# Experts' half pages become pages for at most 32 tokens, with fp32 products on four column groups of the array

## The chip, the cores and the metric

The kernel runs on one core of one Trainium2 chip. The metric is the device time of one execution in microseconds (us); the median of three runs before the change is 1147.6 us (1146.25 to 1148.35).

## What is computed

Three stages follow one another:

- attention over 4 batches, 8 heads, 768 positions, 64 dimensions, where a query sees 4 sink positions and a window of 128;
- a dense layer, `h = x @ w_in`, `g = h * cos(h)`, `g @ w_out`, on 3072 tokens, 512 wide inside and outside and 2048 wide between;
- a mixture of 8 experts with one expert per token: `logits = x @ w_gate + modality_bias[modality_id]`, the expert is the argmax, and `out = gate_w * (relu(x @ w1[e]) @ w2[e])`, with `w1[e]` 512 x 1024 and `w2[e]` 1024 x 512.

All inputs and outputs are float32. How many tokens an expert gets is known only on the chip. For the inputs as they are drawn, the reference sends 1 token to expert 2, 1549 to expert 4 and 1522 to expert 7, and none to the other five.

## The kernel before

Attention and the dense layer are interleaved and fill the first 830 us. The change touches only the experts' stage behind them.

**Pages.** A table computed on the chip (lines 1176 to 1262) cuts each expert's tokens into pages of 256. At most 19 pages exist (`NSUP`, line 99), and the program has code for each of them: `run(T)` (line 1305) nests itself, and each page stands under a condition that it is there. Page 0 and page 1 of the expert that led when it was chosen come first, then the rest of its pages, then the next experts in a ring. Row 2 of the table (line 1244) holds whether a page has more than 128 tokens. If it has, `run(T)` takes the full page, else the half page (`with full.Else()`, line 1353).

**Numbers.** A float32 operand is split into two fp32r parts, high and low, and a product is three fp32r matmuls (high by high, high by low, low by high). The weights of the current expert stand split in SBUF, 8 tiles each `w1h`, `w1l`, `w2h`, `w2l` of 128 x 512; the raw weights of the next expert wait in `rw1` and `rw2`. On the first page of an expert, `on_change` (line 1298) splits them: each split is one ACT copy (L1061) and one DVE subtraction (L148).

**A full page** (256 tokens): 8 blocks of `first_product` (line 1111), each 12 matmuls of 256 columns, relu on ACT (L1118) and the low part on DVE (L145); then `ahead`: the raw weights of the expert after (`reload`, line 1277, DMAs of SP), the next page's tokens transposed and split (`prelude`, line 1099, 8 transposes), and `second_product` (line 1140) for the first 128 tokens, 24 matmuls of 512 columns, between which the next page's `split_w1` stand; then the same product for the other 128 tokens. Each half ends with one ACT scaling by the gate weight (L1149) and one indirect DMA of POOL that scatters 128 rows into the output (L1152); rows that are padding are dropped by their index.

**A half page** (at most 128 tokens): `first_product_half` (line 1121) runs twice, for 512 of the 1024 hidden columns each. There the tokens are the stationary operand (128 columns) and the weights move: 12 matmuls of 512 columns. ACT takes the relu into `h_sb` (L1130), `turn_half` (line 1132) transposes it back in 8 transposes, and ACT (L1137) and DVE (L148) write 8 high and 8 low parts of 128 x 128. `ahead` with `second_product` for the first 128 rows ends the page.

**Order.** From line 1296 on the schedule is manual: every engine runs its instructions in the order in which the program text issues them. Conditions are evaluated by every engine on its own sequencer. On the half page the text says: the four `split_w2` of the first half on ACT and DVE before the first 12 matmuls, the other four before the second 12, then the transposes, the row indices of the page after next on DVE (`rows_ahead`, line 1316, six small operations), `reload`, `prelude` of the next page, and the second product with the next page's eight `split_w1`, the scaling, the gather of the page after next on POOL (`after`, line 1323) and the scatter.

Elsewhere in the kernel there are products in plain fp32, which the compiler issues as two passes, each with its own weight load: `po` in attention writes two column groups of 64 (tile 128*64), `ps` of the first attention pages uses two row groups of 64 (64*128), and `pf` the whole array.

Of the kernel before, what the change touches and what calls it, by code (L numbers as in the profile page):

```python
# [11 lines left out]
F32 = DT.float32  # L12
# [4 lines left out]
AF = mybir.ActivationFunctionType  # L17
ALU = mybir.AluOpType
AX = mybir.AxisListType

P = 128
# [34 lines left out]
WO_LAG = 1  # L56
CONV_A = 0.2
CONV_LEAD = 8


@with_exitstack
def kernel(
# [18 lines left out]
    NT, DM = out.shape  # L81
# [53 lines left out]
    def mm(o, l, r, start, stop):  # L135
        PE.matmul(o, l, r, start=start, stop=stop)  # L136

    def ts(e, o, i, s1, op0, s2=None, op1=None):
        if op1 is None:
            e.tensor_scalar(out=o, in0=i, scalar1=s1, scalar2=None, op0=op0)  # L140
        else:
            e.tensor_scalar(out=o, in0=i, scalar1=s1, scalar2=s2, op0=op0, op1=op1)  # L142
# [4 lines left out]
    def tt(e, o, a, b, op):  # L147
        e.tensor_tensor(out=o, in0=a, in1=b, op=op)  # L148
# [950 lines left out]
    def prelude(T, banks):  # L1099
        i = T % 2  # L1100
        yg = m_yg[i]
        xh, xl = m_x[i]
        for g in range(KD // 2):
            pt = banks[g].rearrange("p (c x) -> p c x", c=2)
            for c in range(2):
                for h in range(2):
                    PE.transpose(pt[:, c, h * P:(h + 1) * P], yg[h][:, (2 * g + c) * P:(2 * g + c + 1) * P], ident)  # L1107
            ACT.activation(out=xh[g], in_=pt, func=AF.Copy)
            tt(DVE, xl[g], pt, xh[g].bitcast(F32), ALU.subtract)
# [8 lines left out]
        ACT.activation(out=hT_h[f], in_=hp, func=AF.Relu)  # L1118
        stt(DVE, hT_l[f], hp, 0.0, hT_h[f].bitcast(F32), ALU.max, ALU.subtract)

    def first_product_half(T, g, hp):

        xh, xl = m_x[T % 2]
        for c in range(KD):
            i, o = divmod(c, 2)
            w = g * KD + c
            mm(hp, xh[i][:, o, 0:P], w1h[w], c == 0, False)
            mm(hp, xh[i][:, o, 0:P], w1l[w], False, False)
            mm(hp, xl[i][:, o, 0:P], w1h[w], False, c == KD - 1)
        ACT.activation(out=h_sb[g], in_=hp, func=AF.Relu)  # L1130

    def turn_half(g, pt):
        for o in range(KD):
            PE.transpose(pt[:, o * P:(o + 1) * P], h_sb[g][:, o * P:(o + 1) * P], ident)
        for o in range(KD):
            f, s = g * KD + o, slice(o * P, (o + 1) * P)
            ACT.activation(out=hT_h[f][:, 0:P], in_=pt[:, s], func=AF.Copy)  # L1137
            tt(DVE, hT_l[f][:, 0:P], pt[:, s], hT_h[f][:, 0:P].bitcast(F32), ALU.subtract)

    def second_product(T, h, yp, between=None, behind=None):  # L1140
        i = T % 2
        s = slice(h * P, (h + 1) * P)
        for f in range(KE):
            mm(yp, hT_h[f][:, s], w2h[f], f == 0, False)
            mm(yp, hT_h[f][:, s], w2l[f], False, False)
            mm(yp, hT_l[f][:, s], w2h[f], False, f == KE - 1)
            if between is not None:
                between(f)
        ACT.activation(out=m_ot[h], in_=yp, func=AF.Copy, scale=m_yg[i][h][:, DM:YC])  # L1149
        if behind is not None:  # L1150
            behind()
        POOL.indirect_dma_start(out=out[:, :], out_offset=bass.IndirectOffsetOnAxis(ap=m_ids[T % 4][:, h:h + 1], axis=0),  # L1152
                                in_=m_ot[h], in_offset=None, bounds_check=NT - 1, oob_is_err=False)
# [87 lines left out]
    ts(DVE, tab[:, 1], page, 0.0, ALU.is_equal)  # L1241
    tt(DVE, tab[:, 1], tab[:, 1], v1_, ALU.mult)
    stt(DVE, g1[:, :, 0], page, -256.0, pct, ALU.mult, ALU.add)
    ts(DVE, tab[:, 2], g1[:, :, 0], float(P), ALU.is_gt)
    tt(DVE, tab[:, 2], tab[:, 2], v1_, ALU.mult)
    ts(DVE, page, page, 2.0, ALU.mult)
    stt(DVE, page, pe_, float(NTI), page, ALU.mult, ALU.add)
# [18 lines left out]
    def maybe(cond):  # L1266
        return tc.If(cond) if cond is not None else ExitStack()
# [9 lines left out]
    def reload(T):  # L1277
        nxt = val(4, T, (ET.SP,), NE - 1)
        has = val(5, T, (ET.SP,), 1)
        load_raw(nxt, has > 0)  # L1280
# [10 lines left out]
        second_product(0, 1, m_y[1], lambda f: prelude(1, m_a) if f == PPF else None, lambda: gather_go(2))  # L1291
    m_h = [ps_h(f"m_h{i}") for i in range(2)]
    m_t = [m_y[1], ps_y(2, "m_t")]
    h_sb = [wpool.tile([P, 512], F32, name=f"h_sb{i}", tag=f"wo{KE + 6 + i}") for i in range(2)]

    ctx.enter_context(tc.manual_schedule())

    def on_change(T, f, split_f):

        if f % 2 == 0:  # L1300
            with tc.If(flags[T, "chg"] > 0):  # L1301
                split_f(f)
                split_f(f + 1)

    def run(T):
        more = T + 1 < NSUP
        cond = None
        if more:
            cond = flags.get((T + 1, "valid"))
            cond = cond > 0 if cond is not None else None  # L1310
            load_flags(T + 1)
        after = None
        cond2 = flags.get((T + 2, "valid"))
        cond2 = cond2 > 0 if cond2 is not None else None

        def rows_ahead():

            if T + 2 < NSUP:
                with maybe(cond2):
                    gather_rows(T + 2, val(3, T + 2, (ET.DVE,), NV - 1))  # L1320

        if T + 2 < NSUP:
            def after():
                with maybe(cond2):
                    gather_go(T + 2)

        def ahead(behind=None):
            if T > 1:
                reload(T)
            if more:  # L1330
                with maybe(cond):
                    prelude(T + 1, m_a)
            second_product(T, 0, m_y[0], (lambda f: on_change(T + 1, f, split_w1)) if more else None, behind)

        def split_ahead(f):
            if T > 1:
                on_change(T, f, split_w2)

        def look_ahead():
            if more:  # L1340
                tc.mark_branch_hint_location(f"full{T + 1}", hint=flags[T + 1, "full"], engines=(ET.PE,))
                if cond is not None:
                    tc.mark_branch_hint_location(f"more{T + 1}", hint=flags[T + 1, "valid"], engines=(ET.Pool, ET.Activation, ET.DVE))

        with tc.If(flags[T, "full"] > 0, preferred_fallthrough_block=True, label=f"full{T}" if T > 1 else None) as full:
            for f in range(KE):
                first_product(T, f, m_h[f % 2][:, 0:256])
                split_ahead(f)
            ahead()
            rows_ahead()  # L1350
            look_ahead()
            second_product(T, 1, m_y[1], None, after)
        with full.Else():
            for g in range(KE // KD):

                for f in range(g * KD, (g + 1) * KD):
                    split_ahead(f)
                first_product_half(T, g, m_h[g])
            for g in range(KE // KD):
                turn_half(g, m_t[g])  # L1360
            look_ahead()
            rows_ahead()
            ahead(after)
        if more and cond is not None:
            with tc.If(cond, preferred_fallthrough_block=True, label=f"more{T + 1}"):
                run(T + 1)
        return more and cond is None
# [40 lines left out]
```

## Time and profile before

| | |
|---|---|
| median of three runs | 1147.6 us |
| the profiled execution, its own time | 1148.82 us |
| its span, first to last instruction | 1147.0 us |
| mean granted TensorE clock over the span | 0.990 of full |
| PE busy | 1096.3 us (96%) |
| DVE busy | 716.0 us (62%) |
| ACT busy | 627.9 us (55%) |

The span is what the engines' records cover; the execution's own time has 1.8 us around it. A row of the timeline gives start and length in us, engine, line, operation, tiles (output from inputs), tile of the array, shape, and how many of a kind were merged; in brackets stand the idle time before it and what ended it. The granted clock is 1.00 at 2.4 GHz and 0.50 at 1.2 GHz.

### The profile page before, as it was taken

The numbers are of one execution on the slowest core, as the hardware profiler recorded it, in microseconds if no ns is written. First come the engines' busy times: TensorE is split into PE (matmuls) and PEld (weight loads), VectorE is DVE, ScalarE is ACT, GpSimd is POOL, SyncE is SP. The second block draws the span as 40 slices with busy tenths as digits, with TensorE's granted clock in tenths as the row PEclk, the third lists the DMA queues.
The fourth block names the chain that finished last, engine by engine and source line by source line (L and its number), as shares of the span: only waits on it lengthen the run. The fifth ranks groups of instructions, "written<-read, shape, count | busy, mean of one in ns | idle before, by whom it ended". The sixth has DMA issues, their size and how long they took to land.

```text
span 1147.0 us, 20828 instructions
## 1 busy us (share of the span) xinstructions
PE 1096.3 (96%) x6504; PEld 939.1 (82%) x6504; DVE 716.0 (62%) x2206; ACT 627.9 (55%) x1283; POOL 225.3 (20%) x275
## 2 busy tenths in 40 slices
PE   5989999999999999999999999999999998999995
PEld 3667778888888888888888889899889997899994
DVE  6678888877877777887787774746742225622210
ACT  4879888766676776666777653434322224522221
POOL 1232223211111121111111112321112211221110
PEclk9989999999999999999999999999999999999998
DMA  6557675433433432342343323623151114111110
GB/s 149 137 179 195 196 217 162 116 86 78 102 89 85 118 83 73 107 91 77 79 114 92 78 75 108 238 77 100 49 203 45 54 55 158 57 55 51 39 40 26
DMA packets 139285, 118.56 MB, mean 103 GB/s; under 512 B 96367, under 2 KB 105583, under 8 KB 139120
## 3 DMA queue, kind: packets, MB, share of 16 engines
q1 hardware_dynamic: 134800, 103.02, 32.1%
q0 software_dynamic: 4320, 13.65, 3.6%
q8 instruction: 65, 1.06, 0.4%
q14 instruction: 100, 0.82, 0.2%
HBM read 151.06 MB, written 19.67 MB: 149 GB/s over the span
## 4 chain that ended last, share of the span: by engine, by line
PE 75%; DVE 12%; DMA 4%; ACT 4%; issue 2%; POOL 1%; SPq 0%; ACTq 0%; POOLq 0%; DVEq 0%
PE hp L136 19%; PE y L640 17%; PE m_y L136 11%; PE m_h L136 10%; PE po L136 5%; PE ps L136 4%; DMA out_dram<-m_ot,m_ids 3%; PE pl L768 1%; DVE pT L148 1%; DVE ch L142 1%; DVE qT L148 1%; PE pt L570 1%; PE m_a L1107 1%; DVE kl L148 1%; DMA cv_in<-in_moe_w_in_dram 1%
## 5 line engine op out<-in xcount | busy, mean ns | idle before, releaser
L148 POOL TENSOR_TENSOR g_l<-ch,g_h 128x384 fp32r<-128x384 f32 x128 | 132.9, 1040 | 552.5 <-ACT g_h L712 513.6
L136 PE MATMUL hp<-xT_h,wi_h 128*128 128x384 f32 x512 | 182.8, 357 | 2.5 <-DVE ch L148 2.5
L136 PE MATMUL hp<-xT_l,wi_h 128*128 128x384 f32 x512 | 175.1, 342 | 0.0
L136 PE MATMUL hp<-xT_h,wi_l 128*128 128x384 f32 x512 | 174.4, 341 | 0.0
L640 PE MATMUL y<-wo,g_h 128*128 128x512 f32 x384 | 157.0, 410 | 0.0
L640 PE MATMUL y<-wo_l,g_h 128*128 128x512 f32 x384 | 155.9, 406 | 0.0
L640 PE MATMUL y<-wo,g_l 128*128 128x512 f32 x384 | 154.7, 403 | 0.2 <-POOL g_l L148 0.2
L702 ACT ACTIVATE ch<-ch,cols 128x384 f32<-128x384 f32 x128 | 78.8, 616 | 118.6 <-DVE ch L145 117.9
L136 PE MATMUL m_y<-wi_h,hT 128*128 128x512 f32 x416 | 133.6, 396 | 0.7 <-ACT m_ot L1149 0.5
L145 DVE SCALAR_TENSOR_TENSOR hT<-m_h,hT 128x256 fp32r<-128x256 f32 x88 | 37.3, 424 | 151.3 <-ACTq L1301 77.7
L136 PEld LDWEIGHTS hp<-xT_h,wi_h 128*128 128x128 f32 x512 | 97.2, 190 | 10.4 <-issue 3.4
L142 DVE TENSOR_SCALAR ch<-hp 128x384 int32<-128x384 f32 x128 | 71.0, 555 | 49.4 <-PE hp L136 38.0
L136 PEld LDWEIGHTS hp<-xT_l,wi_h 128*128 128x128 f32 x512 | 97.3, 190 | 5.5 <-issue 1.9
L136 PEld LDWEIGHTS hp<-xT_h,wi_l 128*128 128x128 f32 x512 | 96.9, 189 | 1.2 <-issue 0.9
L712 ACT ACTIVATE g_h<-ch 128x384 fp32r<-128x384 f32 x128 | 66.4, 520 | 54.0 <-DVE ch L148 42.9
L148 DVE TENSOR_TENSOR ch<-ch,hp 128x384 f32<-128x384 f32 x128 | 70.4, 551 | 38.1 <-ACT ch L702 37.7
L136 PEld LDWEIGHTS m_y<-wi_h,hT 128*128 128x128 f32 x416 | 78.9, 190 | 17.3 <-issue 0.9
L532 ACT ACTIVATE Pb<-Pb,mx 128x272 f32<-128x272 f32 (+1 forms) x168 | 82.8, 494 | 9.1 <-DVE mx L516 8.2
L640 PEld LDWEIGHTS y<-wo,g_l 128*128 128x128 f32 x384 | 72.3, 188 | 14.1 <-POOL g_l L148 0.6
L136 PE MATMUL m_y<-wi_l,hT 128*128 128x512 f32 x208 | 81.6, 392 | 0.0
L1118 ACT ACTIVATE hT<-m_h 128x256 fp32r<-128x256 f32 x88 | 33.7, 383 | 87.4 <-PE m_h L136 82.1
L640 PEld LDWEIGHTS y<-wo,g_h 128*128 128x128 f32 x384 | 72.4, 189 | 10.5 <-issue 2.7
(280 smaller groups left out, 2371.5 us busy)
## 6 DMA issues: line engine op xcount, KB each, us to landing
rw<-in_moe_w_dram SPq DMA_DIRECT2D x112, 512.0 KB
wo_l<-wl_scr SPq DMA_DIRECT2D x122, 256.0 KB
cv_in<-in_moe_w_in_dram SPq DMA_DIRECT2D x16, 512.0 KB
cv_out<-in_moe_w_out_dram SPq DMA_DIRECT2D x16, 512.0 KB
y_scr<-yt SPq DMA_DIRECT2D x24, 256.5 KB
xT_h<-xg_h SPq DMA_DIRECT2D x32, 192.0 KB
xT_l<-xg_l SPq DMA_DIRECT2D x32, 192.0 KB
qn<-in_q_dram SPq DMA_DIRECT2D x56, 96.0 KB
```

The costliest lines, as they stand in the source:

```text
L136: PE.matmul(o, l, r, start=start, stop=stop)
L142: e.tensor_scalar(out=o, in0=i, scalar1=s1, scalar2=s2, op0=op0, op1=op1)
L145: e.scalar_tensor_tensor(out=o, in0=i0, scalar=s, in1=i1, op0=op0, op1=op1)
L148: e.tensor_tensor(out=o, in0=a, in1=b, op=op)
L532: ACT.activation(out=Pb[t][j][:, c0:c1], in_=Pb[t][j][:, c0:c1], func=AF.Exp, scale=-1.0, bias=mx[:, i:i + 1], accum_out=sm[:, i:i + 1])
L570: PE.transpose(pt[:, j, P:2 * P], Pb[t][j][:, SEG:W3], ident)
L640: i = PE.matmul(o, l, r, start=start, stop=stop)
L702: ACT.activation(out=ch, in_=ch, func=AF.Sin, scale=TWO_PI, bias=half_pi)
L712: ACT.activation(out=gh, in_=ch, func=AF.Copy)
L768: return PE.matmul(pl[0][:, 0:NE], yT[:, c, :], wg[:, c, :], start=c == 0, stop=c == KD - 1)
L1107: PE.transpose(pt[:, c, h * P:(h + 1) * P], yg[h][:, (2 * g + c) * P:(2 * g + c + 1) * P], ident)
L1118: ACT.activation(out=hT_h[f], in_=hp, func=AF.Relu)
```

## The change

The limit between the two kinds of page falls from 128 to 32 tokens. A page of at most 32 tokens no longer uses `first_product_half`, `turn_half` and `second_product`. Its tokens (32 columns) are the stationary operand in each of four column groups of the array, the high and low parts of the tokens are added back to float32 on DVE, and the split weights are read as float32 and move in quarters: 256 of the 1024 hidden columns per group in the first product (32 calls), 128 of the 512 output columns per group in the second (64 calls). One relu, two transposes and one copy lie between, and four scalings (two on ACT, two on DVE) behind. The order of the text changes too: `few_first` stands ahead of the splits, `rows_ahead` and half of the next page's `split_w1` move behind the scaling and the scatter, and the gather of the page after next behind the scatter.

```diff
+FEW = 32
+GRP = P // FEW
...
-    def first_product_half(T, g, hp):
+    def few_first(T, hp):
 
         xh, xl = m_x[T % 2]
+        for g in range(KD // 2):
+            tt(DVE, x_few[:, 2 * g:2 * g + 2, :], xh[g][:, :, 0:FEW].bitcast(F32), xl[g][:, :, 0:FEW].bitcast(F32), ALU.add)
         for c in range(KD):
-            i, o = divmod(c, 2)
-            w = g * KD + c
-            mm(hp, xh[i][:, o, 0:P], w1h[w], c == 0, False)
-            mm(hp, xh[i][:, o, 0:P], w1l[w], False, False)
-            mm(hp, xl[i][:, o, 0:P], w1h[w], False, c == KD - 1)
-        ACT.activation(out=h_sb[g], in_=hp, func=AF.Relu)
-
-    def turn_half(g, pt):
-        for o in range(KD):
-            PE.transpose(pt[:, o * P:(o + 1) * P], h_sb[g][:, o * P:(o + 1) * P], ident)
-        for o in range(KD):
-            f, s = g * KD + o, slice(o * P, (o + 1) * P)
-            ACT.activation(out=hT_h[f][:, 0:P], in_=pt[:, s], func=AF.Copy)
-            tt(DVE, hT_l[f][:, 0:P], pt[:, s], hT_h[f][:, 0:P].bitcast(F32), ALU.subtract)
+            for ws in (w1h, w1l):
+                for j in range(GRP):
+                    w = ws[j // 2 * KD + c][:, j % 2 * 256:j % 2 * 256 + 256].bitcast(F32)
+                    mm(hp[j * FEW:(j + 1) * FEW, 0:256], x_few[:, c, :], w, c == 0 and ws is w1h, c == KD - 1 and ws is w1l)
+
+    def few_turn(hp, pt):
+        ACT.activation(out=h_few, in_=hp[:, 0:256], func=AF.Relu)
+        for o in range(2):
+            PE.transpose(pt[:, o * P:(o + 1) * P], h_few[:, o * P:(o + 1) * P], ident)
+        DVE.tensor_copy(ht_few, pt[:, 0:256])
+
+    def few_second(T, yp):
+        for f in range(KE):
+            ht = ht_few[:, f % 2 * P + f // 2 * FEW:f % 2 * P + (f // 2 + 1) * FEW]
+            for ws in (w2h, w2l):
+                for j in range(GRP):
+                    w = ws[f][:, j * P:(j + 1) * P].bitcast(F32)
+                    mm(yp[j * FEW:(j + 1) * FEW, 0:P], ht, w, f == 0 and ws is w2h, f == KE - 1 and ws is w2l)
+
+    def few_out(T, yp):
+        pr = m_yg[T % 2][0][0:FEW, DM:YC]
+        for j in range(GRP):
+            o, r = m_ot[0][0:FEW, j * P:(j + 1) * P], yp[j * FEW:(j + 1) * FEW, 0:P]
+            if j % 2 == 0:
+                ACT.activation(out=o, in_=r, func=AF.Copy, scale=pr)
+            else:
+                ts(DVE, o, r, pr, ALU.mult)
+        POOL.indirect_dma_start(out=out[:, :], out_offset=bass.IndirectOffsetOnAxis(ap=m_ids[T % 4][:, 0:1], axis=0),
+                                in_=m_ot[0], in_offset=None, bounds_check=NT - 1, oob_is_err=False)
...
-    ts(DVE, tab[:, 2], g1[:, :, 0], float(P), ALU.is_gt)
+    ts(DVE, tab[:, 2], g1[:, :, 0], float(FEW), ALU.is_gt)
...
-    h_sb = [wpool.tile([P, 512], F32, name=f"h_sb{i}", tag=f"wo{KE + 6 + i}") for i in range(2)]
+    h_few, ht_few = [wpool.tile([P, 256], F32, name=f"{n_}_few", tag=f"wo{KE + 6 + i}") for i, n_ in enumerate(("h", "ht"))]
+    x_few = fin.tile([P, KD, FEW], F32, name="x_few")
...
         with full.Else():
-            for g in range(KE // KD):
-
-                for f in range(g * KD, (g + 1) * KD):
-                    split_ahead(f)
-                first_product_half(T, g, m_h[g])
-            for g in range(KE // KD):
-                turn_half(g, m_t[g])
+            few_first(T, m_h[0])
+            for f in range(KD):
+                split_ahead(f)
+            few_turn(m_h[0], m_t[1])
+            for f in range(KD, KE):
+                split_ahead(f)
             look_ahead()
+            if T > 1:
+                reload(T)
+            if more:
+                with maybe(cond):
+                    prelude(T + 1, m_a)
+            few_second(T, m_y[0])
+            for f in range(KD if more else 0):
+                on_change(T + 1, f, split_w1)
+            few_out(T, m_y[0])
             rows_ahead()
-            ahead(after)
+            if after is not None:
+                after()
+            for f in range(KD, KE if more else 0):
+                on_change(T + 1, f, split_w1)
```

## Rows read from the trace of the kernel before

**Rows 1.** The chain that ended last, in order of time (start, us, what); its end
```profile
962.39 4.35 issue
...
981.95 11.90 PE m_h L136 x96
...
1101.36 36.30 DMA out_dram<-m_ot,m_ids
```

**Rows 2.** Stretches: length, busy us of PE PEld DVE ACT POOL, clock, DMA share, GB/s
```profile
937.91:961.23 23.32, 23.31 (x153) 21.07 (x151) 10.34 (x24) 9.70 (x20) 4.08 (x4) 1.00 0.21 65
961.23:982.00 20.77, 16.18 (x66) 13.29 (x67) 11.69 (x29) 13.05 (x29) 2.03 (x2) 0.84 0.59 212
971.19:978.02 6.83, 5.83 (x20) 5.15 (x21) 4.19 (x16) 4.45 (x14) 0.00 (x0) 0.50 0.80 270
1122.34:1136.45 14.11, 12.51 (x57) 9.78 (x56) 2.24 (x8) 4.57 (x12) 0.98 (x1) 1.00 0.07 26
```

**Rows 3.** DMA packets while the last scatter lands (1136 to 1147) and after 988.75
```profile
DMA packets 85, 0.08 MB, mean 7 GB/s; under 512 B 73, under 2 KB 73, under 8 KB 80
...
q0 software_dynamic: 80, 0.03, 0.9%
...
DMA packets 74, 0.00 MB, mean 2 GB/s; under 512 B 73, under 2 KB 73, under 8 KB 74
```

**Rows 4.** Timeline of page 13, the last one
```profile
1121.95 0.39 PE L136 MATMUL m_y<-wi_h,hT 128*128 128x512 f32 x1
1122.68 0.47 PE L136 MATMUL m_h<-wi_h,m_x 128*128 128x512 f32 x1 [0.34 <-issue]
...
1135.28 0.39 PE L136 MATMUL m_y<-wi_h,hT 128*128 128x512 f32 x1
1135.76 0.69 ACT L1149 ACTIVATE m_ot<-m_y,m_yg 128x512 f32<-128x512 f32 x1 [2.51 <-PE m_y L136]
```

**Rows 5.** Timeline of PE: fp32 products on two column groups, one group, whole array
```profile
307.59 0.54 PE L136 MATMUL po<-sp,vs_n 128*64 128x384 f32 x2
...
308.29 1.47 PE L136 MATMUL po<-pT,vn 128*64 128x128 f32 x16
...
308.29 0.39 PE L136 MATMUL po<-pT,vn 128*64 128x128 f32 x4
...
119.30 0.72 PE L136 MATMUL ps<-kT,qT 64*128 64x272 f32 x2
...
101.16 0.60 PE L136 MATMUL pf<-ident,pb_x 128*128 128x128 f32 x4
```

**Rows 6.** Groups by form (line, engine, operation, shapes, count, busy us, mean ns, idle before)
```profile
L136 PE MATMUL po<-pT,vn 128*64 128x128 f32 x168 | 16.7, 273 | 0.0
...
L1118 ACT ACTIVATE hT<-m_h 128x256 fp32r<-128x256 f32 x88 | 33.7, 383 | 87.4 <-PE m_h L136 82.1 <-DVEq L1301 2.8 <-issue 1.3
...
L145 DVE SCALAR_TENSOR_TENSOR hT<-m_h,hT 128x256 fp32r<-128x256 f32 x88 | 37.3, 424 | 151.3 <-ACTq L1301 77.7 <-ACT hT L1118 73.6
```

**Rows 7.** Timeline of page 6 and the start of page 7
```profile
962.58 0.47 PE L136 MATMUL m_h<-wi_h,m_xT_h 128*128 128x512 f32 x1 [1.35 <-ACT m_ot L1149]
...
966.90 2.19 ACT L1061 ACTIVATE wi_h<-rw 128x512 fp32r<-128x512 f32 x4 [4.96 <-issue]
...
967.57 5.06 DVE L148 TENSOR_TENSOR wi_l<-rw,wi_h 128x512 fp32r<-128x512 f32 x8 [9.94 <-ACT wi_h L1061]
...
969.63 0.66 PE L1134 MATMUL m_y<-ident,h_sb 128*128 128x128 f32 x4 [1.33 <-ACT h_sb L1130]
...
972.20 1.11 PE L1134 MATMUL m_t<-ident,h_sb 128*128 128x128 f32 x4 [1.91 <-ACT h_sb L1130]
...
974.67 0.78 PE L136 MATMUL m_y<-wi_h,hT 128*128 128x512 f32 x1
...
978.21 0.16 DVE L145 SCALAR_TENSOR_TENSOR m_ids<-m_it,m_ix 128x2 uint32<-128x2 f32 x1
...
981.78 0.40 PE L136 MATMUL m_h<-m_x,wi_h 128*128 128x256 f32 x2
```

More of the change, by code (lines that the diff above doesn't have):

```diff
@@ L1325, in after, with ahead @@
                     gather_go(T + 2)
-        def ahead(behind=None):
+        def ahead():
             if T > 1:
@@ L1332, in ahead @@
                     prelude(T + 1, m_a)
-            second_product(T, 0, m_y[0], (lambda f: on_change(T + 1, f, split_w1)) if more else None, behind)
+            second_product(T, 0, m_y[0], (lambda f: on_change(T + 1, f, split_w1)) if more else None)
         def split_ahead(f):
```

## The prediction

> **What bounds the kernel now.** I read the chain of waits first: in the experts' stage it is almost wholly PE, page after page (page 7's first product is one link of 11.90 us), and it ends with 36.3 us that the view gives to the last scatter, behind which the last page lies [rows 1]. Two stretches look different. Around 962 the chain is not PE for 4.35 us but "issue". The table of stretches says the same: a full page (937.91 to 961.23) keeps PE busy for 23.31 of 23.32 us, page 6 (961.23 to 982.00) for 16.18 of 20.77, with the clock at half for 6.83 us, and page 13 (1122.34 to the end of its scaling at 1136.45) for 12.51 of 14.11 [rows 2]. These two are the half pages, and the change can act on nothing else.
>
> **Do both pages become small ones?** Yes. The last scatter has 80 packets, of which 7 are over 2 KB, and the queue moved 0.03 MB in all: some 13 rows of 2 KB, not 128. After 988.75, where page 6's scatter ends, one packet over 512 B is left [rows 3]. The reference's routing agrees: expert 7's 1522 tokens are pages 0 to 5, expert 2's one token is page 6, and expert 4's 1549 are pages 7 to 13, the last with 13 tokens. No page holds 33 to 128 tokens, so none becomes a full page.
>
> **The price of a product.** A plain fp32 call is two passes. On the whole array four passes of 128 columns take 0.60 us, the last one 0.27 from its start, so a pass takes (0.60 - 0.27) / 3 = 0.11 us per 128 columns, 0.22 per 256 [rows 5, 6]. The passes of one call on one group follow each other: two of 272 columns take 0.72 us. Two column groups run side by side: two passes of 384 columns (0.33 each by that price) are both over after 0.54 us, where one after the other they would take 0.83, and 16 passes, half of 128 and half of 256 columns (the row bears the shape of the first), are over after 1.47 us, 1.30 without the drain of the last, where one after the other they would need 8 x 0.11 + 8 x 0.22 = 2.64 [rows 5]. Four groups are not in the trace. Bounds: as wide as two (each pass then counts half), or four wide (a quarter). I take four, because the second group costs no visible time in the rows, and keep two for the range. Then few_first, 32 calls or 64 passes of 256 columns, is 16 x 0.22 = 3.5 us; few_second, 64 calls or 128 passes of 128 columns, is 32 x 0.11 = 3.5 us. Each replaces 24 matmuls of 512 columns, some 5.5 us (the second product of page 13 ends its last start at 1135.28). A drain of some 0.17 us follows each product, as 0.27 for a pass of 0.11 shows [rows 4, 6].
>
> The Trainium skill, TensorE: Matmul & The Clock Gate (Part 3, The mechanism), says that matmuls start and end strictly in program order. By that rule a call's second pass would hold back the next group's first one, no more than two passes would ever overlap, and each product would cost 7.0 us instead of 3.5: that is the first rival below. The trace disagrees at the start of a series: two passes end within 0.54 us of the first start [rows 5], and they can't be those of one call.
>
> **Page 13, all of it on the path to the end.** From the end of page 12's product: branch 0.34 (kept, though the splits' branches now stand behind the product), few_first 3.5 + 0.17, relu 0.38 of 128 x 256 on ACT, two transposes 0.11 + 0.27, copy on DVE as the 128 x 256 row 0.42, few_second 3.5 + 0.17, two scalings each on ACT and DVE, some 0.5 together (one of 512 columns took 0.69), and four or five hand-overs of 0.05: 9.6 us [rows 4, 6]. Before: 14.1. **Gain 4.5 us**, since POOL's scatter waits for the scaling alone and all behind it (1147.0 - 1136.45 = 10.55 us to the end of the span) stays. POOL's conditions, which now stand behind the scatter, lie beside the wait for its landing. The two small DVE additions for x_few come before PE needs them: DVE has been idle since page 13's tokens were split. ACT's eight relu and transpose copies and DVE's eight subtractions go; they were hidden but for the first.
>
> **Page 6, with the splits of a new expert.** PE finishes few_first at 962.58 + 3.7 = 966.3, but nobody takes it: ACT comes out of its branch at 966.90 (an idle of 4.96 "issue" that the change leaves alone) and has four splits ahead of the relu, until 969.1 [rows 7]. So this product's gain is lost in a wait. Relu 969.5, transposes 969.95; DVE has its four subtractions behind it at 970.1 and copies until 970.5. Page 7's eight transposes, at 0.11 and a drain, end at 971.2. The clock: PE will have idled 3.2 us, as it idled 1.33 + 1.91 = 3.24 us in two parts before, when the records show half clock from 971.19 on [rows 2, 7]; I take the same here, and that it comes back after the products have run for as long as before, 978.02 - 974.67 = 3.35 us [rows 2, 7]. Half of few_second then runs at 0.22 per step (15 steps), 17 steps at 0.11 = 1.9: it ends at 976.6. The splits of w2 keep ahead of it (DVE is through at 972.95).
>
> Next late is DVE. ACT splits until 971.65; then come page 7's tokens, two copies on ACT and, at the price of two subtractions (5.06 / 8 = 0.63 each, 0.6 in a row), 1.3 us on DVE to 974.3, and four subtractions of w1 to 976.8 [rows 7], just in time for page 7's first block. Then stand on DVE, in order, two scalings (0.6), the row indices (register loads, which I put at 0.8, and six operations of 0.17 [rows 7]) and four more subtractions (2.4): the first hT_l of page 7 is done at 982.2. PE has two product banks, so its third block (a block is an eighth of some 11.6 us, 1.45) waits for it from 976.8 + 2.9 = 979.7: a new stall of 2.5 us, and 0.25 at the fourth block. ACT, with four splits behind its scalings, is ready sooner. Page 7's first product therefore starts 981.78 - 976.8 = 5.0 us sooner and waits 2.75 longer. **Gain 2.2 us**, which carries through, since from there every page is PE to the end. Bounds: full clock throughout gives 1.4 more; the clock lost again in the new stall costs up to 1.7 (half of 3.4), held down until 978.02 another 1.6. The gather for page 8 comes some 2 us earlier on POOL than before and isn't needed until 990; reload's DMAs on SP wait for the w2 splits as before, half a microsecond later, and are needed 8 us later.
>
> **Sum.** 4.5 + 2.2 = 6.7 us of the profiled 1148.8, which is 1.2 above the median; against the median 1147.6 - 6.7 = **1140.9 us**. About 0.2% (2.3 us) is what a measurement can tell from no change.
>
> **Rivals.** (1) Two groups wide. Products cost 7.0 each. Page 13: 9.6 + 7.0 = 16.6 against 14.1, a loss of 2.5. Page 6: few_first ends at 969.8, relu, transposes and page 7's transposes until 971.6, few_second until 978.8, page 7 starts 2.9 sooner and waits 2.75 longer, a gain of 0.1. Together 1150.0, slower than before; with half clock in page 7, 1151.7. It decides at a width under about 2.5 groups, where page 13 alone gains no more than 1.5 us. For it: no row has more than two. Against: the second group was free.
> (2) PE isn't fed fast enough. few_second is 256 instructions with its weight loads; the densest stretch of passes in the rows, four passes of 128 columns on two groups (two steps of 0.11, with four loads), is 0.027 us per instruction [rows 5]. At that pace few_second takes 6.9 us: page 13 gains 1.1, page 6 ends 1.7 later and gains 0.5, together 1146.0. For it: no denser stretch. Against: that one is paced by the array itself.
> (3) Page 7's stall and the clock eat page 6's gain: 0.5 to -1.1 instead of 2.2, so 1142.6 to 1144.2. For it: the stall is as long as the idle that cost the clock before.
> (4) The groups don't run side by side at all: 14 us per product, where 9.6 + 21 = 30.6 stands against 14.1; page 7 would start at 992.4, 10.6 later, and wait 2.75 more: 1147.6 + 16.5 + 13.4 = 1177.5. The rows for two groups speak against it.
>
> **How the numbers follow.** The forecast has 0.60 (1139 to 1142.6), rival 3 has 0.14, rival 1 0.13, rival 2 0.09, rival 4 and a stall in code loading that I don't see 0.04. Faster by over 0.2% is below 1145.3: 0.60 and most of rival 3, less 0.02 for what I don't see in either, 0.71. Same is 1145.3 to 1149.9: rival 2, over half of rival 1 (its price sits at the limit) and 0.01 of rival 3, 0.17. Slower: 0.12. The forecast's own range is 1139 (full clock, 1.4 more, and the branch saved) to 1142.6; with rivals 3, 2 and most of 1 the range is 1138.7 to 1150.0.
>
> **What would show it.** In the changed profile: in page 13, eight passes within some 0.25 us where now two to four stand, first product of about 3.7 us, last scaling some 4.5 us closer to page 12's end; in page 6, PE idle from 966.3 to 969.5, half clock from about 971; in page 7, an idle of 2 to 3 us before the third block, ended by DVE hT. Passes that start in pairs would prove rival 1, evenly spread starts at 0.05 us rival 2. The sum is wrong if page 7 has no stall, or if ACT reaches page 6 at another time.

## The result, and the profile after

The change made the kernel slower. The median went from 1146.92 us (1145.25 to 1148.35, four runs on the same chip) to 1161.05 us (1159.43 to 1161.95, four runs), a ratio on record of 1.0113 with a 95% interval of 1.0098 to 1.0128 (the two medians alone give 1.0123). The forecast was 1140.9 us, with a range that ended at 1150.0. Medians and ratios in this document leave out two executions that ran slower throughout at a lower clock, one of `few_act` (1204.25 us) and one of the kernel before beside it (1769.58 us).

The profiled execution took 1160.85 us, its span is 1159.1 us. The same view as [rows 2], for the changed kernel: page 5, page 6, a stretch of half clock in it, page 7, pages 7 to 12 (from the first scaling of page 7 to the last of page 12), page 13, the half clock in it, and what follows the last scaling.

```profile
936.77:960.06 23.29, 23.29 (x153) 21.05 (x151) 10.71 (x26) 9.74 (x20) 4.08 (x4) 1.00 0.20 61
960.06:981.60 21.54, 11.48 (x204) 7.68 (x203) 9.08 (x16) 8.75 (x17) 2.03 (x2) 0.76 0.60 207
969.11:972.47 3.36, 3.36 (x33) 1.91 (x36) 0.00 (x0) 0.00 (x0) 0.00 (x0) 0.50 0.85 241
981.60:1003.30 21.70, 19.36 (x133) 17.93 (x134) 14.25 (x36) 11.36 (x24) 3.98 (x3) 1.00 0.11 29
1002.60:1130.80 128.20, 123.12 (x784) 110.69 (x782) 27.37 (x76) 28.46 (x62) 21.39 (x21) 1.00 0.15 46
1130.71:1147.37 16.66, 10.52 (x194) 6.85 (x194) 1.11 (x3) 1.79 (x4) 0.98 (x1) 0.80 0.07 23
1134.12:1139.67 5.55, 5.52 (x53) 2.92 (x57) 0.00 (x0) 0.00 (x0) 0.00 (x0) 0.50 0.04 9
1147.37:1159.07 11.70, 0.00 (x0) 0.00 (x0) 0.00 (x1) 0.00 (x0) 0.99 (x1) 0.61 0.03 8
```

The row to stop at is the fifth. Pages 7 to 12 are all full and run not one instruction of the new code, yet they take 128.20 us. The kernel before needs 122.08 for the same 784 matmuls:

```profile
1000.30:1122.38 122.08, 122.04 (x784) 111.15 (x782) 27.04 (x74) 28.35 (x61) 21.37 (x21) 1.00 0.15 48
```

PE was never idle there before; now it idles 5.1 us, and its records are 1.1 us longer. The two small pages lost as well, where both should have gained: from page 5's last scaling to page 7's first 42.45 us (39.04 before), page 13 from page 12's last scaling to the end of its own 16.57 (14.07 before), and the rest of the span 11.70 (10.60). With the 6.12 of the full pages that is 3.41 + 6.12 + 2.50 + 1.10 = 13.1 us; the stretch up to page 5's last scaling was 1.1 shorter in this execution, so the spans differ by 12.0.

Where the full pages lose it is in a view that the busy times leave out: the branches of the condition "full page", by duration. Columns: engine, operation, count, shortest / median / longest in ns, first and last start in us. First the changed kernel, pages 7 to 12, then the kernel before:

```profile
L1365 PEldq COMPARE_BRANCH  x11: 71/3392/4186, 1003.7 to 1126.8; - x11
```

```profile
L1345 PEldq COMPARE_BRANCH  x11: 70/169/317, 1001.4 to 1118.4; - x11
```

Five of each are tests at a page's start (70 to 83 ns). The other six are the jumps with which a full page leaves its own code and skips the small page's: 0.17 to 0.32 us before, 3.4 to 4.2 us now, on PE's sequencer. The DMA view of the jump that starts at 1003.7 shows what arrives while it lasts, one packet of 16 KB on the queue "instruction":

```profile
q0 software_dynamic: 101, 0.35, 32.6%
q8 instruction: 1, 0.02, 1.8%
```

Each of the six jumps has such a packet, which starts 0.9 to 1.0 us behind the jump's start. In the same stretch of the kernel before (1001.4 to 1004.9) that queue has no packet. Over pages 7 to 12 it has 16 in the changed kernel and 10 in the kernel before, one more for each of the six jumps:

```profile
q8 instruction: 16, 0.26, 0.9%
```

```profile
q8 instruction: 10, 0.16, 0.6%
```

In page 7 PE's last matmul ends 4.2 us after the jump begins, so most of a jump is hidden behind matmuls that are queued: the six take 22.1 us together, and 6.1 show.

Page 6 and its successor, timeline of the changed kernel (as [rows 7]):

```profile
965.54 1.08 PE L138 MATMUL m_h<-wi_h,x_few 128*32 128x256 f32 x8 [5.48 <-issue]
965.89 2.19 ACT L1063 ACTIVATE wi_h<-rw 128x512 fp32r<-128x512 f32 x4 [5.05 <-issue]
969.11 0.65 PE L138 MATMUL m_h<-wi_l,x_few 128*32 128x256 f32 x4 [2.11 <-issue]
974.07 0.38 ACT L1135 ACTIVATE h_few<-m_h 128x256 f32<-128x256 f32 x1 [5.99 <-issue]
981.60 0.50 PE L138 MATMUL m_h<-m_x,wi_h 128*128 128x256 f32 x2 [1.65 <-issue]
987.07 0.50 PE L138 MATMUL m_h<-m_x,wi_h 128*128 128x256 f32 x2 [2.34 <-DVE hT L147]
```

PE stands 5.48 us before the page's first matmul and 2.11 us in the middle of the product, both put down to "issue", a wait for nothing that the profile shows. Ahead of the first matmul PE's sequencer is held by the branch into the page, 4.91 us from 960.4; in the middle there is no branch, but a packet of 16 KB on q8 (966.4 to 967.7), so that wait is put down to code by inference. Page 13 (as [rows 4]) opens the same way, though the view names ACT's sequencer for its 3.44 us, and then runs its first product at half clock:

```profile
1134.15 1.08 PE L138 MATMUL m_h<-wi_h,x_few 128*32 128x256 f32 x8 [3.44 <-ACTq L1321]
1134.97 1.11 PE L138 MATMUL m_h<-wi_l,x_few 128*32 128x256 f32 x8
...
1140.64 0.38 ACT L1135 ACTIVATE h_few<-m_h 128x256 f32<-128x256 f32 x1 [9.16 <-PE m_h L138]
...
1142.04 0.43 PE L138 MATMUL m_y<-wi_h,ht_few 128*32 128x128 f32 x8 [0.52 <-DVEq L1321]
1142.28 0.40 PE L138 MATMUL m_y<-wi_l,ht_few 128*32 128x128 f32 x8
...
1145.86 0.36 ACT L1153 ACTIVATE m_ot<-m_y,m_yg 32x128 f32<-32x128 f32 x1 [4.83 <-PE m_y L138]
1146.25 0.34 DVE L142 TENSOR_SCALAR m_ot<-m_y,m_yg 32x128 f32<-32x128 f32 x1 [4.27 <-ACT m_ot L1153]
1146.63 0.36 ACT L1153 ACTIVATE m_ot<-m_y,m_yg 32x128 f32<-32x128 f32 x1 [0.41 <-DVE m_ot L142]
1147.02 0.35 DVE L142 TENSOR_SCALAR m_ot<-m_y,m_yg 32x128 f32<-32x128 f32 x1 [0.43 <-ACT m_ot L1153]
```

### The profile page after: what moved, and what is told of

It reads as the page before. It is cut to its first block, busy times and chain, and to the rows that moved or that the text cites. A ratio compares the mean times of both kernels' runs of the same rounds, so it can differ in the third digit from the quotient of the medians.

```text
span 1159.1 us, 21349 instructions
## 1 busy us (share of the span) xinstructions
PE 1089.5 (94%) x6780; PEld 928.1 (80%) x6780; DVE 714.3 (62%) x2200; ACT 623.3 (54%) x1267; POOL 225.8 (19%) x275
## 4 chain that ended last, share of the span: by engine, by line
PE 72%; DVE 12%; issue 7%; ACT 4%; DMA 2%; POOL 1%; SPq 0%; POOLq 0%; DVEq 0%; ACTq 0%
PE hp L138 19%; PE y L642 18%; PE m_y L138 9%; PE m_h L138 9%; PE po L138 5%; PE ps L138 5%; PE pl L770 1%; DVE pT L150 1%; DVE ch L144 1%; DVE qT L150 1%; DVE kl L150 1%; DMA out_dram<-m_ot,m_ids 1%; PE pt L572 1%; DVE cv_a L147 1%; ACT Pb L534 1%
## 5 line engine op out<-in xcount | busy, mean ns | idle before, releaser
L138 PE MATMUL m_y<-wi_h,hT 128*128 128x512 f32 x384 | 122.1, 393 | 0.5 <-ACT m_ot L1168 0.5
L138 PEld LDWEIGHTS m_y<-wi_h,hT 128*128 128x128 f32 x384 | 72.0, 188 | 15.4 <-issue 0.9
L642 PEld LDWEIGHTS y<-wo_l,g_h 128*128 128x128 f32 x384 | 72.5, 189 | 9.1 <-DMA wo_l<-wl_scr 1.1
```

Of the source, the lines that this page charges most:

```text
L642: i = PE.matmul(o, l, r, start=start, stop=stop)
```

## The experiments

Theory C: PE's instructions come in pieces by DMA, and the longer code of the small pages makes every jump over it, and every entry into it, wait for a piece. Rival O: the new order of the small pages, or their transfers, does it. The table collects all kernels by stretch, each from the scalings in its timeline: A from page 5's last scaling to page 7's first, B from there to page 12's last, C from there to the end of page 13's last, D to the end of the span.

| kernel | A | B | C | D | median us, ratio to before (95%) |
|---|---|---|---|---|---|
| before | 39.04 | 122.08 | 14.07 | 10.60 | 1146.92 |
| after | 42.45 | 128.20 | 16.57 | 11.70 | 1161.05, 1.0113 (1.0098 to 1.0128) |
| pad_else | 39.10 | 128.20 | 14.25 | 10.99 | 1153.28, 1.0046 (1.0032 to 1.0059) |
| pad_356 | 38.86 | 124.10 | 14.62 | 10.97 | 1150.15 (one run) |
| pad_260 | 38.80 | 122.10 | 14.51 | 11.24 | 1146.45 (one run) |
| few_6_13 | 37.96 | 122.18 | 11.55 | 11.66 | 1144.83, 0.9977 (0.9966 to 0.9989) |
| half_5_12 | 39.49 | 127.81 | 10.83 | 11.69 | 1150.83 (one run) |
| few_fall | 38.51 | 122.15 | 10.46 | 12.78 | 1144.98, 0.9973 (0.9960 to 0.9987) |
| before_fall | 35.88 | 122.09 | 13.46 | 13.02 | 1146.23, 0.9983 (0.9969 to 0.9996) |
| few_tail | 36.48 | 122.08 | 12.50 | 10.27 | 1142.02, 0.9943 (0.9926 to 0.9961) |
| few_act | 37.20 | 122.09 | 12.44 | 10.15 | 1142.58, 0.9947 (0.9934 to 0.9960) |
| few_two | 37.20 | 122.08 | 11.95 | 10.06 | 1140.29 (one run) |
| few_mix | 38.05 | 122.11 | 13.76 | 10.76 | 1145.21, 0.9987 (0.9972 to 1.0002) |

The kernel before took 1147.55 to 1148.94 us in the median beside these runs. A row's stretches are those of one execution; where the code is the same they differ by up to 0.7 us (A of few_tail, few_act and few_two, D of the kernel before and pad_260).

**The jumped code alone.**

```diff
-        for c in range(KD):
+        for c in list(range(KD)) * times:
...
-                first_product_half(T, g, m_h[g])
+                first_product_half(T, g, m_h[g], 1 if T in (6, 13) else 7)
```

> The kernel before, in which the half page of every page except 6 and 13 issues its 24 matmuls of the first product seven times. These pages are all full or absent, so nothing more is executed; only the stretch of PE instructions that a full page jumps over at its end grows from about 164 to about 451, the length it has in the changed kernel (448). Theory C (code): a jump over the long stretch lands on instructions that are not loaded, 3.4 to 4.2 us instead of 0.17 to 0.33, of which some 0.5 to 2.3 us per page shows. Pages 7 to 12 then lose 5 to 7 us together, and the jump of page 5 delays the branch into page 6 by up to 2 us: 1152 to 1156 us. Rival O (order): the full pages of the changed kernel lose time to the new order of its small pages or to its DMAs: 1147 us, no change here.

B is 128.20 us, to the hundredth the changed kernel's, with not one instruction more executed:

```profile
998.56:1126.76 128.20, 123.10 (x784) 110.69 (x782) 27.02 (x74) 28.34 (x61) 21.37 (x21) 1.00 0.14 47
```

Five of the six jumps took 3.3 to 4.2 us, the sixth 0.43:

```profile
L1345 PEldq COMPARE_BRANCH  x11: 71/428/4184, 999.7 to 1122.8; - x11
```

Queue q8 has 17 packets in this stretch, against 10 in the kernel before; only PE's code was changed, so q8 brings PE's code. Rival O is out for the full pages: the length of code that PE skips is enough. A stayed as it was, against the expectation, because here the jumps of pages 1 to 5 were still short (0.3 us); the changed kernel's are 0.29 to 0.39 us on pages 1 to 3, 1.30 on page 4 and over 3.3 from page 5 on.

**How long is too long.** The same with 3 and with 5 in place of 7.

> As pad_else, with the first product's matmuls issued three times instead of seven: the stretch jumped over has 260 PE instructions (164 in the kernel before, 451 in pad_else). Instructions come in pieces of 16 KB, and 16 KB are 256 of them at 64 bytes each. If what counts is whether the target lies in the piece that is loaded ahead, the jumps are free or nearly so: pages 7 to 12 take 122.1 to 123 us from the scaling of page 6's successor to page 12's last, jumps under 0.5 us. If the cost grows with the length, they take 122.1 + 6.1 x 96 / 287 = 124.1 us.

> As pad_260, with the matmuls issued five times: 356 PE instructions. If the piece loaded ahead counts, some pages' jumps are long (over 3 us) and others short (under 0.5 us), pages 7 to 12 take 123 to 127 us. If the cost grows with the length, every jump costs some, and they take 122.1 + 6.1 x 192 / 287 = 126.2 us.

The branches of pages 7 to 12, first with 260 instructions to skip, then with 356:

```profile
L1345 PEldq COMPARE_BRANCH  x11: 70/287/326, 997.9 to 1114.9; - x11
```

```profile
L1345 PEldq COMPARE_BRANCH  x11: 70/292/3839, 999.8 to 1118.8; - x11
```

With 260 every jump is free, B is 122.10. With 356 one jump of the six takes 3.84 us and the others 0.43 at most, and B is 2.0 longer. So the cost is not proportional to the length: on these pages a jump takes 0.43 us at most, or over 3.2. The Trainium skill, Advanced Engine Details and Errata (ISA Cache), says that an engine's code is held in lines of 16 KB, 256 instructions. The packets of 16 KB agree, and the three lengths fit a target that is free when it lies in the piece already loaded ahead. The compiled programs bear this out for the jumps out of the full pages. Cut them in pieces of 256 instructions (branch labels not counted, which leaves about 243 of the 260 and 338 of the 356; the first cut fitted once for all kernels): of 121 such jumps, in all kernels of the table but few_fall and before_fall, the 98 whose target lies in the same piece or the next took 0.43 us at most, and of the 23 that skip a whole piece 22 took 0.62 to 4.19 us. The one that doesn't fit is the sixth in pad_else. The fit was made afterwards and no run tested it, so the rule remains argued; the branches into pages 6 and 13 don't follow it, they took 1.4 to 5.2 us in all these kernels.

**The short code on all pages but two.**

```diff
         with full.Else():
-            few_page()
+            few_page() if T in (6, 13) else half_page()
```

Here `few_page` is the body that the change put there, `half_page` the one that it took away.

> The changed kernel, in which only pages 6 and 13 carry the code for few tokens; the other pages carry the old half page behind their condition, which they never take. Theory C: the jumps of the full pages are 0.17 to 0.33 us again, pages 7 to 12 give back about 6 us, and page 6 is entered up to 2 us earlier: 1152.5 to 1155.5 us. What is left against the kernel before, some 6 us, is the price of the two small pages themselves. Rival O: 1160 to 1162 us as the changed kernel.

B is 122.18 as expected, but the kernel came out at 1144.83 us, 7.7 us below the expected range and faster than the one before. I had counted only the full pages' 6 us as the code's. A (-4.5 us against the changed kernel) and C (-5.0) belong to it as well: page 13's first product starts with no idle ahead of it (a hole of 0.88 us follows in its middle), and runs eight passes of 256 columns in 0.43 us where the changed kernel, at half clock, needs 0.85.

**Only the pages ahead of the two small ones.**

```diff
-            few_page() if T in (6, 13) else half_page()
+            half_page() if T in (5, 12) else few_page()
```

> The changed kernel with the old half page behind the condition of pages 5 and 12 alone (never taken there), so that only the full pages just ahead of the two small pages have a short stretch to jump over. Theory C: the small pages lose because PE comes late to their branch, held up in the jump at the end of the page ahead: from page 5's last scaling to page 7's first the profile shows 38 us as in few_6_13, not 42.4; page 13 takes 11.5 to 12.5 us, not 16.6, its first product at full clock. Pages 8 to 11 still pay 4 to 6 us in their jumps. In all 1150 to 1153 us. Rival: the small pages lose in their own code, whatever stands ahead of them: 42.4 and 16.6 us stay, 1159 to 1161 us.

B still pays (127.81), and page 13 is cured (10.83) though its own code is that of the changed kernel. So page 13, and page 6 for the greater part, lost by what stands ahead of them. The branch into page 13 takes about as long in both kernels, 2.05 us in the changed one and 1.93 here. In the changed kernel the jump out of page 12 (3.66 us) holds PE's sequencer, and the branch starts at 1131.8, when the last matmul of page 12 has ended (1130.71). Here it starts at 1124.5, and matmuls are queued until 1126.45. The two branches of the changed kernel, then both in this run:

```profile
L1365 PEldq COMPARE_BRANCH  x1: 3662/3662/3662, 1126.8 to 1126.8; - x1
L1365 PEldq COMPARE_BRANCH  x1: 2053/2053/2053, 1131.8 to 1131.8; - x1
```

```profile
L1420 PEldq COMPARE_BRANCH  x2: 326/1129/1932, 1122.5 to 1124.5; - x2
```

Timeline of PE at page 13's start in this run:

```profile
1126.06 0.39 PE L138 MATMUL m_y<-wi_h,hT 128*128 128x512 f32 x1
1126.65 0.64 PE L138 MATMUL m_h<-wi_h,x_few 128*32 128x256 f32 x8 [0.21 <-issue]
1127.08 0.64 PE L138 MATMUL m_h<-wi_l,x_few 128*32 128x256 f32 x8
```

For page 6 two thirds came back (39.49, expected 38).

**Entry without a jump.**

```diff
-preferred_fallthrough_block=True
+preferred_fallthrough_block=T not in (6, 13)
```

This on few_6_13, and on the kernel before:

> As the run before it, with the code for few tokens of pages 6 and 13 placed directly behind the branch, and the full page's code behind it, so that these two pages are entered without a jump. Theory C: page 13's first product starts some 0.4 us behind page 12's last matmul instead of 3.4, PE keeps its full clock there (four passes of 256 columns in 0.21 us, not 0.43), page 13 gains 5 to 6 us; page 6 is entered 4 us earlier on PE and on ACT, and its first product is not broken in two, 5 to 10 us, less up to 3 us for the jump over the full page's code at its end. 1138 to 1146 us. Rival S: the pace of 0.43 us for four passes is that of four column groups, not of the clock, and the idle before the first product is the reading of conditions: 1150 to 1154 us.

> The kernel before, with the half page of pages 6 and 13 placed directly behind the branch, the full page's code behind it. Theory C: the chain's 4.35 us of issue in front of page 6 goes, 3 to 5 us of it gained, less up to 3 us for the jump over the full page's code at page 6's end; page 13 (0.34 us of idle) gains nothing: 1142 to 1147 us. Theory against it: ACT and DVE with their 24 splits and copies bound page 6, and nothing is gained: 1147 us. The difference to the run before it is what the products on four column groups are worth when neither kernel pays for its jumps: 0 to 5 us in their favour by the prediction's sum less the scalings' hand-overs.

In few_fall page 13 begins without a gap and C falls to 10.46; rival S is out, the four groups run at eight passes in 0.43 us when the clock is 1.00. PE ends page 6 sooner by 3.5 us, but now the jump over the full page's code comes at its end, and page 7 waits for that:

```profile
978.63 0.79 PE L138 MATMUL m_h<-m_x,wi_h 128*128 128x256 f32 x2 [4.90 <-issue]
```

D grows too: PE's last branch takes 5.2 us, in few_6_13 3.8. The sum is that of few_6_13. In before_fall page 6 gains 3.2 of the 4.35 us of "issue" that [rows 1] show, so these too came from the jump to its code, and D gives 2.4 back. ACT's 4.96 us [rows 7] go with them:

```profile
962.10 2.21 ACT L1061 ACTIVATE wi_h<-rw 128x512 fp32r<-128x512 f32 x4 [0.63 <-ACT m_ot L1149]
```

**Order behind the second product.**

```diff
-            for f in range(KD if more else 0):
+            for f in range(KE if more else 0):
                 on_change(T + 1, f, split_w1)
-            few_out(T, m_y[0])
             rows_ahead()
-            if after is not None:
-                after()
-            for f in range(KD, KE if more else 0):
-                on_change(T + 1, f, split_w1)
+            few_out(T, m_y[0], after)
```

> As few_6_13, with the order behind the second product of a small page changed: all eight of the next page's conditional splits and the row indices stand ahead of the scalings, and the gather of the page after next between scalings and scatter, as in the kernel before. Theory P (POOL): the end of few_6_13 is 1.1 us later behind its last scaling than before, because POOL reads its conditions only behind the scatter, longer than the scatter takes to land; it goes back to 10.6 us. Theory D (DVE): page 7 waits 1.3 us in its third block for splits that stand on DVE behind the scalings and the row indices; that wait goes. Both: 2.4 us less than few_6_13 on the same chip (0.9979 of it). If neither holds, the same time.

Both held: D is 10.27 us, A 1.5 less (0.8 in few_act and few_two, with the same code there), and the stall in page 7's third block is gone. C was 0.95 longer, with "issue" in the middle of page 13's first product again (1.26 us). At 0.9943 of the kernel before this is the fastest version that computes everything, together with few_act below, from which it can't be told. It singles out pages 6 and 13; which pages are small depends on the inputs, so on others its time would not be this one. Page 13's own stretch (length, busy times, clock, as above) shows full clock, with PE idle for 0.39 us ahead of the first product and 1.26 us in it:

```profile
1117.43:1129.97 12.54, 8.20 (x195) 5.80 (x194) 1.11 (x3) 1.79 (x4) 0.98 (x1) 1.00 0.09 29
```

POOL's waits at the end show why. First the kernel before, then the changed one, the sequencer's waits for semaphores and its conditions (min/median/max ns, first and last start):

```profile
L1365 POOLq EVENT_SEMAPHORE  x5: 17/43/1328, 1138.2 to 1139.8; - x5
L1365 POOLq COMPARE_BRANCH  x2: 49/58/68, 1137.7 to 1141.2; - x2
```

```profile
L1396 POOLq EVENT_SEMAPHORE  x5: 17/42/43, 1151.8 to 1152.2; - x5
L1396 POOLq COMPARE_BRANCH  x2: 49/58/68, 1151.3 to 1153.6; - x2
```

Before, POOL reaches the end 1.3 us behind the last scaling (1136.45) and then waits 1.33 us for the scatter. Now it reaches it 3.9 us behind (1147.37), and nothing is left to wait for. On the way lie two entries of the DMA queue's bookkeeping (INC_SWDGE_SEM, 1.2 us each) and the conditions of the gather and the splits; before, it was one such entry.

**The scalings.**

```diff
-            if j % 2 == 0:
+            if True:
```

```diff
-            o, r = m_ot[0][0:FEW, j * P:(j + 1) * P], yp[j * FEW:(j + 1) * FEW, 0:P]
+            o, r = m_ot[j % 2][0:FEW, j * P:(j + 1) * P], yp[j * FEW:(j + 1) * FEW, 0:P]
```

> As few_tail, with all four scalings of a small page on ACT, so that none waits for the other engine. In few_tail ACT and DVE take turns: four scalings of 0.34 to 0.36 us begin 0.39 us apart and take 1.51 us. If an engine's own scalings begin sooner behind one another than 0.39 (ACT's splits begin 0.55 apart where one takes 0.62), the four take 1.0 to 1.3 us: 0.2 to 0.5 us less than few_tail, 1141.5 to 1142 us. If they stand one behind the other, the same 1.5 us and the same time.

> As few_tail, but DVE's two scalings write into another tile, the second of the two output tiles; the scatter sends the first one only, so half the columns of the small pages' rows are left out. If the turns that ACT and DVE take come from both writing one tile, the two engines now work side by side and the four scalings take 0.7 to 0.9 us instead of 1.51. If they come from both reading one bank of product sums, or from the engines themselves, 1.5 us stays.

On ACT alone the four took 1.52 us, one behind the other, as the second half of the expectation says. With two output tiles ACT and DVE still took turns, 1127.33 behind 1126.94, 1127.71 behind that:

```profile
1127.33 0.34 DVE L142 TENSOR_SCALAR m_ot<-m_y,m_yg 32x128 f32<-32x128 f32 x1 [4.29 <-ACT m_ot L1172]
1127.71 0.36 ACT L1172 ACTIVATE m_ot<-m_y,m_yg 32x128 f32<-32x128 f32 x1 [0.41 <-DVE m_ot L142]
```

So it is not the tile they write. What they still share is the bank of sums that both read, and each is released by the other's end. The Trainium skill, PSUM — Partial Sum Buffer (PSUM bank collisions raise a hardware error), says that two engines may use one bank at once in different quarters of 32 partitions, as the four groups here lie; the program orders them all the same, and no run here lets them overlap.

**A version without page numbers.** The order of few_tail on every page, the second product as the half page has it:

```diff
-                for j in range(GRP):
-                    w = ws[f][:, j * P:(j + 1) * P].bitcast(F32)
-                    mm(yp[j * FEW:(j + 1) * FEW, 0:P], ht, w, f == 0 and ws is w2h, f == KE - 1 and ws is w2l)
+            mm(yp[0:FEW], hh, w2h[f], f == 0, False)
+            mm(yp[0:FEW], hh, w2l[f], False, False)
+            mm(yp[0:FEW], hl, w2h[f], False, f == KE - 1)
```

> The changed kernel on every page, with the order of few_tail, and a small page's second product as the half page has it: 24 fp32r matmuls of 512 columns with 32 tokens stationary, into one 32 x 512 tile with one scaling; the first product stays on four column groups in fp32. The stretch that a full page jumps over is 242 PE instructions instead of 448. Theory C: the jumps are short again, pages 7 to 12 take 122.1 us and not 128.2. The second product costs 1.9 us more than on four groups, one scaling instead of four with hand-overs 0.8 us less, the wait for instructions inside the page goes (0.9 us in page 13 of few_6_13): 1141 to 1145 us without a page singled out. If 242 instructions are too many for a free jump: 1147 to 1151 us.

With 242 instructions to skip, B is 122.11, as expected. But page 6 was entered late (a branch of 5.23 us, 3.76 of PE idle), and page 13 had 1.84 us of "issue" in its first product, a wait that the expectation had as gone. The time, 1145.21 us, lies 0.2 above the expected range and can't be told from the kernel before (the interval reaches 1.0002).

## Why the prediction was wrong

**"The change can act on nothing else"** than the two half pages: this step failed. It counted instructions where they run, not where they stand. The small pages' code grew from about 164 to 448 PE instructions (counted in the compiled program, branch labels included) on each of 18 pages, and the full pages paid 6.1 us to skip it (shown by pad_else and by few_6_13). The late entries and the half clock behind them cost the small pages another 9.5 us (A and C of few_6_13 against the changed kernel). The clue was in my own rows: 4.35 us of "issue" on the chain [rows 1] and 4.96 on ACT [rows 7] where the kernel before jumps into page 6. I took them as fixed; before_fall shows that 3.2 us of the one and 4.3 of the other go when the page is entered without a jump. "A stall in code loading that I don't see" had shared 0.04 with rival 4. The two signs by which I would have called the sum wrong, no stall in page 7 or another time for ACT, both came out as forecast: neither looked at code. Longer code is a cost like any other and should have had a term and a bound.

**Price of a product**: right. Four groups run side by side: eight passes of 256 columns in 0.43 us at full clock (0.22 for four, as forecast), and few_second took 3.70 us, forecast 3.67. That ends rivals 1 and 4. (By these prices page 13 gains 1.5 us at a width of 2.8 groups, not at 2.5 as the prediction has it.) Rival 2 had named 0.027 us per instruction as a limit; 256 of them went in 3.70 us, 0.014 each. But its idea, that PE isn't fed, was near what happened: not the pace of single instructions held PE up, but the pieces they come in.

**Page 13**: forecast 9.6 us from the last matmul of page 12, measured 16.66. Entry 3.44 instead of 0.34 (+3.1, code); first product 6.4 instead of 3.67 (+2.7: its clock was 0.50 for 5.55 us, behind 3.44 us of idle; my price was one at 1.00); the relu, transposes and copy 1.5 (forecast 1.4); second product as forecast; scalings 1.6 instead of 0.55 (+1.1, one behind the other). In few_6_13, with neither late entry nor half clock, page 13 gained 2.5 of the forecast 4.5 us.

**"Lie beside the wait for its landing"**, of POOL's conditions behind the scatter: wrong by 1.1 us. They and the queue's bookkeeping take longer than the landing; few_tail took it back.

**Page 6**: two pieces that do not depend on few_first came as forecast. ACT left its branch at 965.89 (forecast 966.90, in an execution 1.1 us ahead); page 7 stalled 2.34 us before its third block, ended by DVE's hT (forecast 2.5). What failed is few_first, ready at 973.96 instead of about 965: 5.48 and 2.11 us of "issue", and half clock until 972.45. The clock had fallen before the product began, while PE stood idle:

```profile
962.21:972.45 10.24, 4.80 (x41) 2.49 (x45) 2.50 (x4) 2.19 (x4) 1.02 (x1) 0.50 0.68 227
```

ACT, which I had made the late one, waited 5.99 us for it. A second piece was missing from the sum, and in it no branch waits for code: PE stood 1.65 us between few_second's last matmul (979.94) and page 7's first (981.60 above), where I had 0.2. Its sequencer was then busy with the tests of page 7's splits, which the change puts behind the product, and with two register loads of 0.31 us:

```profile
L1321 PEldq COMPARE_BRANCH  x8: 65/120/180, 979.1 to 980.3; - x8
L1283 PEldq TENSOR_LOAD <-tab_i x2: 306/308/309, 980.6 to 981.0; - x2
```

In the kernel before these stand between matmuls, and page 7 starts with no idle [rows 7]; few_tail, with all the tests behind the product, still loses 1.72 us there.

With the code out of the way and the order mended, few_tail gains 4.5 us by the stretches and 5.5 in the median, against 6.7 forecast for the same products. The mechanism that I priced was there; the one that I didn't price was worth over twice the forecast gain, with the other sign: few_6_13 against the changed kernel gives 4.5 + 6.0 + 5.0 = 15.5 us by A to C.

## What to carry to other kernels

In a program with branches, count the instructions of the code that is skipped as well as of that which runs: on this kernel a PE jump over up to 260 was free, and one over 448 took 3.4 to 4.2 us on pages 5 and 7 to 12, of which about 1 us a page was not hidden, even where nothing new was executed. "Issue" idle at a branch is a hint of it, but no proof: the 1.65 us ahead of page 7 were tests. The branch's own duration and the packets of the instruction queue tell the two apart. When a product is split into more, smaller calls, ask how often its code stands in the program, and put an engine's conditions ahead of its last transfer, so that it has none left to evaluate when the transfer lands.

## What the hardware showed that I had not expected

- PE's code came in packets of 16 KB, and a jump out of a full page that waited for one took 3.3 to 4.2 us on pages 7 to 12; there the changed kernel loads 16 packets where the one before loads 10. ACT showed 5 us of "issue" on its way into page 6 in both kernels [rows 7], and 0.63 us in before_fall.
- Straight code seems to run dry too: few_first, 64 passes with their weight loads and no branch among them, was interrupted for 0.9 to 2.2 us in few_6_13, few_tail and few_mix. In each case a packet on q8 landed 1.2 to 1.7 us before PE went on; that PE waited for it is inferred.
- In page 13 of the changed kernel, behind 3.44 us of idle, PE ran at clock 0.50 for 5.55 us; in few_tail, behind idles of 0.39 and 1.26 us, the clock stayed at 1.00 through the page.
